# Moving the second batch's scores behind the first products of block 0, in a hand-written order of a sparse attention and feed-forward kernel

## The chip, the cores and the metric

The kernel runs on one core of a Trainium2 chip. The metric is the device time of one execution in microseconds (us); the time of a version is the median of its runs. The engines of the core are TensorE (PE, matrix products), VectorE (DVE), ScalarE (ACT), GpSimd (POOL) and SyncE (SP, here only an issuer of transfers).

## The reference

Sparse attention of 8 batches, 8 heads, 576 tokens of 64 numbers, and then a feed-forward layer on the 4608 tokens of 512 numbers. All is float32.

```python
scores = scale * np.matmul(q, k.transpose(0, 1, 3, 2))
mask_local = (rel >= 0) & (rel < stride)                 # heads 0 to 3
mask_strided = (rel >= 0) & (pos[None, :] % stride == pos[:, None] % stride)   # heads 4 to 7
attn = softmax(np.where(masks, scores, -1e9))
x = np.matmul(attn, v).transpose(0, 2, 1, 3).reshape(B * S, H * D)
h = x @ w_in                                             # 512 x 2048
g = h * (1.0 / (1.0 + np.exp(-h)))
return g @ w_out                                         # 2048 x 512
```

## The kernel before, in words

**Tiling.** The 4608 tokens are cut in nine blocks of 512. A batch's attention is cut in six groups (three of local heads, three of strided heads); group 0 to 5 belong to the first batch, 6 to 11 to the second. Block 0 needs the first batch only. Float32 products of the feed-forward layer are made of three float32r products of split operands (high times high, high times low, low times high).

**Order.** For block 0 every engine's order is written out by hand in the string `PLAN` (line 133), which `Steps.follow` (line 188) reads word by word; each word issues the instructions of one step on one engine. An engine works through its own words in this order and waits where a word needs something that isn't there yet. The words that matter here, with the group or chunk as their number:

- `k` loads keys and queries of a group (line 373, SP queue), `v` its values, `p` a piece of the raw weights into a staging tile (lines 342 and 347).
- `S` makes the scores of a group on PE (line 471; 24 float32 products for a local group, 16 for a strided one, each of which shows as two MATMULs in the trace), `M` adds the mask and takes the maxima on DVE (line 511), `E` the exponentials on ACT (line 529), `R` and `N` sum and scale, `T` transposes on PE (line 554), `P` copies that out (line 558), `O` multiplies with the values (lines 615, 620), `B` copies the result into the block's input x (lines 675, 691).
- `H` and `L` split x into a high and a low part (lines 708, 712), four quarters `00` to `03`.
- `a`, `j`, `b`, `d` turn a raw weight piece into its high and low parts: `a` on ACT (lines 299, 304), `j` on DVE (line 310), `b` on either (line 355), `d` on DVE (line 359).
- `h` and `i` are the first and second half of the products of a chunk of 128 hidden features (line 720, six products of 128 x 512 each); `t` the tanh on ACT (line 730), `g` the gate on DVE (line 752), `w` and `l` the split of the result (lines 760, 764), `o` the output products (line 779).
- `~n` issues idle products: `n` times 128 columns of the identity matrix with itself, into a PSUM bank that nobody reads (line 888).

```python
    def idle(n):
        bank = ps.tile([P, 512], F32, name="ps")
        for i in range(0, n, 4):
            wide = min(4, n - i)
            nc.tensor.matmul(
                bank[:, : wide * P].rearrange("p (i c) -> p i c", c=P), ident,
                ident.unsqueeze(1).broadcast_to([P, wide, P]), start=True, stop=True,
            )
```

**Places.** PSUM has eight banks, four in the ring `ps` and four in `po`. From `ps` a group's scores take two banks until its `M` has read them, a chunk's `h` takes one until its `g` has read it, and idle products take one. A taker gets the bank that has been free the longest. Keys and queries of the second batch lie in two places only (`KBUFS = 2`): groups 6, 8 and 10 use the same place, so `k8` has to wait for `S6` and `k10` for `S8` (in `attention_steps`, `writes=[k_place]`).

Of the kernel before, what the change touches and what calls it, by code (L numbers as in the profile page):

```python
# [132 lines left out]
PLAN = """  # L133
k0 k1 k2 v0 ~7 S0 v1 M0 k4 E0 k3 v2 C0 ~1 S1 k5 M1 E1 ~3 S2 M2 p1 E2 v5 T0 P0.D R1 ~7 S4 O0 R0
M4 E4 Q0 k6 C1 v3 v4 T1 P1.D R2 S3 M3 E3 X0 B0.D a1 T2 P2.D O1 p0 C2 Q1 R4 N4.P S5 M5 k7 O2 X1
Q2 B1.A R3 N3.D S6 k8 j1 T4 P4.A E5 H00.D p3 p4 X2 B2.A M6 T3 P3.D a0 L00.P H01.A O4 p5 p2 O3
b1.D B4 R5 N5.D d1 j0 b0.A L01.P T5 P5.D S8 M8 k10 d0 p6 B3 H02.D L02 O5 B5 H03.D L03 a3 j3
b3.D E6 S7 M7 h0 h1 p7 R6 v7 d3 a5 j5 i0 t0 g0 a2 j2 p9 i1 b5.A d5 w0.D t1 g1 b2.A d2 h2 p11
S10 l0 i2 a6 j6 v6 h3 a7 j7 o0 a4 i3 b6.D w1.D b7.A p8 j4 d7 t2 g2 h4 b4.A d4 l1 o1 k12 p13 a11
N6 p10 w2.A l2 V6 i4 d6 o2 p12 a9 j9 E8 a8 j11 k9 M10 t3 g3 R8 b9.A d9 h5 p15 O6 b11.A d11 a13  # L140
t4 g4 p17 v8 j13 i5 w3.A l3 h6 a10 j10 E10 j8 a12 N8 b8.D d8 o3 p14 w4.A a15 V8 b10.A d10 p16
# [2209 lines left out]
```

## Time and profile before

| | us |
|---|---|
| median of 3 runs | 820.31 (820.23 to 820.51) |
| the profiled execution, its own time | 824.26 |
| its span, first to last instruction | 822.0 |
| PE busy | 811.3 |
| DVE busy | 638.5 |
| ACT busy | 557.5 |
| POOL busy | 74.3 |

The trace's times count from the first instruction of the profiled execution. A row of a timeline gives the start, the length, the engine, the line, what is done and how often, and in brackets the idle time of the engine ahead of it with what ended it; "issue" there is a wait for nothing that the profile shows. The lengths of two neighbouring instructions overlap, so the pitch from one start to the next is the better price of a repeated instruction.

### The profile page before, as it was taken

Reading aid. Unit: us, or ns where it says so; the run is one execution under the profiler, and the core shown is the slowest. Engines: PE = TensorE matmul, PEld = TensorE weight load, DVE = VectorE, ACT = ScalarE, POOL = GpSimd, SP = SyncE. Lnnn points to the kernel's source line nnn. Section 1 sums busy time; section 2 is a strip of 40 time slices with the busy share of each in tenths; the row PEclk is TensorE's granted clock in tenths of the full one; section 3 lists DMA queues with packets and bytes.
Section 4 is the critical chain, followed back from the end, with each engine's and each line's share of the span. In section 5 each row is a group of like instructions: output and inputs, shape, how many; then the busy total and the mean of one; then the engine's idle time right before and its main releaser. Section 6 shows DMA issues by size and latency. Waiting matters only on the chain.

```text
span 822.0 us, 19441 instructions
## 1 busy us (share of the span) xinstructions
PE 811.3 (99%) x7041; PEld 686.5 (84%) x7041; DVE 638.5 (78%) x1571; ACT 557.5 (68%) x1560; POOL 74.3 (9%) x122
## 2 busy tenths in 40 slices
PE   8899999999999999999999999999999999999998
PEld 5688878888898889898988888888888888888887
DVE  6799897787677778786778779676799964789754
ACT  7799876566687678777787769887555624545551
POOL 6300003784000000000000000000000000000000
PEclk9899999999999999999999999999999999999999
DMA  8787354566787876888677877876667697767676
GB/s 270 254 276 253 111 187 127 203 222 237 265 266 252 263 243 210 250 265 264 198 234 247 264 241 242 256 203 181 194 191 219 193 238 227 194 196 194 192 217 156
DMA packets 139007, 182.78 MB, mean 222 GB/s; under 512 B 29408, under 2 KB 82272, under 8 KB 138912
## 3 DMA queue, kind: packets, MB, share of 16 engines
q1 hardware_dynamic: 137392, 180.82, 71.4%
q8 instruction: 56, 0.92, 0.5%
q10 hardware_dynamic: 1520, 0.72, 0.3%
q14 instruction: 39, 0.32, 0.1%
HBM read 142.70 MB, written 38.80 MB: 221 GB/s over the span
## 4 chain that ended last, share of the span: by engine, by line
PE 97%; POOL 1%; issue 1%; DVE 0%; POOLq 0%
PE ps L1549 33%; PE po L779 27%; PE po L2103 13%; PE ps L720 11%; PE ps L2103 4%; PE ps L635 3%; PE po L2232 1%; PE ps L471 1%; PE ps L462 1%; PE po L620 0%; PE po L635 0%; POOL v L399 0%; POOL mask_strided L240 0%; POOL mask__94 L240 0%; PE po L554 0%
## 5 line engine op out<-in xcount | busy, mean ns | idle before, releaser
L1549 PE MATMUL ps<-xop,w 128*128 128x256 f32 (+1 forms) x1152 | 185.5, 310 | 0.0
L1549 PEld LDWEIGHTS ps<-xop,w 128*128 128x128 f32 x1152 | 165.6, 190 | 16.3
L529 ACT ACTIVATE sm<-sm,sums 128x54 f32<-128x54 f32 (+2 forms) x320 | 109.2, 346 | 3.5 <-DVE sums L511 3.4
L720 PE MATMUL ps<-xop,w 128*128 128x512 f32 x384 | 96.5, 400 | 0.0
L1549 PE MATMUL ps<-w,w 128*128 128x512 f32 x384 | 93.7, 389 | 0.0
L779 PE MATMUL po<-w,ghi 128*128 128x512 f32 x280 | 87.1, 392 | 0.0
L720 PEld LDWEIGHTS ps<-xop,w 128*128 128x128 f32 x384 | 72.8, 192 | 15.8
L1549 PEld LDWEIGHTS ps<-w,w 128*128 128x128 f32 x384 | 72.0, 188 | 14.9
L764 DVE TENSOR_TENSOR glo<-th,ghi 128x512 fp32r<-128x512 f32 x80 | 59.3, 743 | 12.4 <-ACT ghi L760 10.5
L529 ACT ACTIVATION_READ_ACCUMULATOR sm<-sm,sums 128x1 f32 x320 | 61.4, 192 | 0.0
L779 PEld LDWEIGHTS po<-w,ghi 128*128 128x128 f32 x280 | 50.4, 189 | 8.9 <-ACT ghi L760 0.2
L760 ACT CAST ghi<-th 128x512 fp32r<-128x512 f32 x78 | 48.3, 621 | 11.8 <-DVE th L752 7.0
L779 PE MATMUL po<-w,glo 128*128 128x512 f32 x140 | 54.6, 390 | 0.0
L779 PE MATMUL po<-stage,ghi 128*128 128x512 f32 x160 | 50.5, 397 | 0.0
L2103 PE MATMUL po<-stage,w 128*128 128x512 f32 x210 | 49.2, 389 | 0.0
L2103 PEld LDWEIGHTS po<-stage,w 128*128 128x128 f32 x210 | 39.4, 188 | 8.2
L602 ACT COPY pt<-sm 32x192 f32<-32x192 f32 (+1 forms) x102 | 36.9, 362 | 5.5 <-DVE sm L594 3.5
L489 POOL MEMSET sm<- 128x80 f32 (+1 forms) x18 | 2.9, 161 | 411.8 <-ACT pt L602 335.0
L1564 ACT ACTIVATE th<-sm 128x512 f32<-128x512 f32 x30 | 18.9, 632 | 29.7 <-DVE sm L1812 24.4
L1942 DVE TENSOR_TENSOR w<-ps,w 128x512 f32<-128x512 f32 x33 | 22.7, 688 | 20.3 <-PE ps L1549 16.3
L2103 PE MATMUL po<-v,w 128*128 128x512 f32 x162 | 38.3, 389 | 0.0
L779 PE MATMUL po<-v,ghi 128*128 128x512 f32 x120 | 38.0, 398 | 0.0
(275 smaller groups left out, 1639.5 us busy)
## 6 DMA issues: line engine op xcount, KB each, us to landing
w<-sums SPq DMA_DIRECT2D x232, 256.0 KB, 3.0
w<-osums SPq DMA_DIRECT2D x104, 256.0 KB, 2.9
sums<-xop SPq DMA_DIRECT2D x16, 512.0 KB, 2.8
osums<-stage SPq DMA_DIRECT2D x16, 512.0 KB, 4.7
v<-vt SPq DMA_DIRECT2D x21, 384.0 KB, 5.3
stage<-w_out SPq DMA_DIRECT2D x14, 512.0 KB, 4.6
k<-kqt SPq DMA_DIRECT2D x14, 477.0 KB, 5.6
stage<-w_in SPq DMA_DIRECT2D x12, 512.0 KB, 4.6
```

The source lines that it names most:

```text
L462: nc.tensor.matmul(self.pss[h][rows, c * WIDE : (c + 1) * WIDE], kbd[at, 1, g.q0[t] : g.q0[t] + 2 * STRIDE], kbd[at, 0, g.k0[t] : g.k0[t] ...
L529: nc.scalar.activation(out=self.s_sb[:, c, h], in_=self.s_sb[:, c, h], func=AF.Exp, bias=self.peaks[:, c, h : h + 1], scale=-1.0, accum_ou ...
L602: nc.scalar.copy(out=self.pt[to, odd], in_=of)
L635: nc.tensor.matmul(self.pso[p][h * D : (h + 1) * D, i * size : (i + 1) * size], vbd[at, 2 * i + h], moved, start=True, stop=True,)
L720: nc.tensor.matmul(ph, weight(0, wi, fc)[:, cc // 2, cc % 2 * P : (cc % 2 + 1) * P], x[xi][cc], start=(cc, n) == (0, 0), stop=(cc, n) == ( ...
L760: copy[engine](out=g[0][:, cols], in_=th[:, cols])
L764: either[engine].tensor_sub(out=g[1][:, cols], in0=th[:, cols], in1=g[0][:, cols].bitcast(F32))
L779: nc.tensor.matmul(po[tt], g[gi][:, cols], weight(1, wi, fc), start=first and n == 0, stop=last and n == 2,)
L1549: nc.tensor.matmul(bank[:, : right.shape[-1]], left(wi, kt), right[:, kt, xi], start=first and (kt, n) == (0, 0), stop=(kt, n) == (1, 2), ...
L1564: nc.scalar.activation(out=th[:, cols], in_=h, func=AF.Tanh, scale=0.5)
L1942: nc.vector.tensor_add(out=to, in0=of(), in1=to)
L2103: nc.tensor.matmul(bank(name, key, m), left[:, wi, m * P : (m + 1) * P], right[xi], start=first and (j, i) == (0, 0), stop=(j, i) == (FH - ...
```

## The change

Two `S`/`M`/`k` triples and one `S`/`M` pair move in `PLAN`, and two idle words are added; no function changes. `S6` is replaced in its old place by `~2` and goes, with `M6` and `k8`, behind `h0`. `S7 M7` goes from ahead of `h0` to behind `i1`. `S8 M8 k10` goes from ahead of `O5` to behind `g1`, and `~4` is put ahead of `O5`. `j3`, `b3.D`, `E6`, `i0` and `i1` change places with their neighbours a little. PE's order becomes `~2 T4 X2 T3 O4 O3 T5 ~4 O5 h0 S6 h1 i0 i1 S7 S8 h2 S10`; before it was `S6 T4 X2 T3 O4 O3 T5 S8 O5 S7 h0 h1 i0 i1 h2 S10`.

```diff
-Q2 B1.A R3 N3.D S6 k8 j1 T4 P4.A E5 H00.D p3 p4 X2 B2.A M6 T3 P3.D a0 L00.P H01.A O4 p5 p2 O3
-b1.D B4 R5 N5.D d1 j0 b0.A L01.P T5 P5.D S8 M8 k10 d0 p6 B3 H02.D L02 O5 B5 H03.D L03 a3 j3
-b3.D E6 S7 M7 h0 h1 p7 R6 v7 d3 a5 j5 i0 t0 g0 a2 j2 p9 i1 b5.A d5 w0.D t1 g1 b2.A d2 h2 p11
+Q2 B1.A R3 N3.D ~2 j1 T4 P4.A E5 H00.D p3 p4 X2 B2.A T3 P3.D a0 L00.P H01.A O4 p5 p2 O3
+b1.D B4 R5 N5.D d1 j0 b0.A L01.P T5 P5.D d0 p6 B3 H02.D L02 ~4 O5 B5 H03.D L03 a3
+h0 S6 M6 k8 j3
+b3.D E6 h1 p7 R6 v7 d3 i0
+a5 j5 t0 g0 i1 S7 M7 a2 j2 p9 b5.A d5 w0.D t1 g1 S8 M8 k10 b2.A d2 h2 p11
 S10 l0 i2 a6 j6 v6 h3 a7 j7 o0 a4 i3 b6.D w1.D b7.A p8 j4 d7 t2 g2 h4 b4.A d4 l1 o1 k12 p13 a11
```

## Rows read from the trace of the kernel before

**Rows 1.** The page: span, busy times of the engines, PE's instruction queue
```profile
span 822.0 us, 19441 instructions
...
PE 811.3 (99%) x7041; PEld 686.5 (84%) x7041; DVE 638.5 (78%) x1571; ACT 557.5 (68%) x1560; POOL 74.3 (9%) x122
...
q8 instruction: 56, 0.92, 0.5%
```

**Rows 2.** Busy time in a stretch: PE, PEld, DVE, ACT, POOL, clock, DMA share, GB/s
```profile
40.00:140.00 100.00, 100.00 (x873) 80.71 (x872) 92.38 (x245) 84.80 (x235) 3.85 (x4) 1.00 0.58 187
```

**Rows 3.** Timeline of PE, 9 to 40 us
```profile
9.25 1.67 PE L888 MATMUL ps<-ident 128*128 128x512 f32 x4
...
16.97 0.35 PE L471 MATMUL ps<-k 64*64 64x64 f32 x8 [1.26 <-issue]
...
18.38 0.72 PE L471 MATMUL ps<-k 64*32 64x64 f32 x48
...
22.16 1.89 PE L620 MATMUL po<-pt,v 64*64 64x54 f32 x57 [0.87 <-issue]
...
24.46 0.72 PE L471 MATMUL ps<-k 64*32 64x64 f32 x48
25.57 0.75 PE L620 MATMUL po<-pt,v 64*64 64x54 f32 x18 [0.39 <-ACT xb L675]
28.69 0.35 PE L620 MATMUL po<-pt,v 64*64 64x54 f32 x2 [2.37 <-issue]
...
30.05 9.31 PE L720 MATMUL ps<-xop,w 128*128 128x512 f32 x30
39.30 0.72 PE L471 MATMUL ps<-k 64*32 64x64 f32 x48
```

**Rows 4.** Busy time in stretches around the stall; the clock is third from the right
```profile
27.00:28.00 1.00, 0.00 (x0) 0.00 (x0) 0.97 (x2) 0.00 (x0) 0.88 (x3) 0.98 1.05 360
...
34.00:35.00 1.00, 1.00 (x4) 0.80 (x3) 0.94 (x2) 0.15 (x1) 0.00 (x0) 0.61 0.12 44
```

**Rows 5.** Chain of work that ended last: six products at the full clock
```profile
51.17 1.36 PE ps L720 x6
```

**Rows 6.** Timeline of DVE, 24 to 34 us
```profile
26.25 0.69 DVE L359 TENSOR_TENSOR w<-stage,w 128x512 fp32r<-128x512 f32 x1
...
27.37 0.69 DVE L712 TENSOR_TENSOR xop<-xb,xop 128x512 fp32r<-128x512 f32 x1
...
32.23 0.21 DVE L511 CUSTOM_DVE_ANT_0 sm<-ps,mask_strided 128x64 f32<-128x64 f32 x1
...
33.38 0.17 DVE L544 TENSOR_SCALAR sums<-sums 128x6 f32<-128x6 f32 x1
```

**Rows 7.** Timeline of POOL, the low part of the second quarter of x
```profile
24.40 1.75 POOL L712 TENSOR_TENSOR xop<-xb,xop 128x512 fp32r<-128x512 f32 x1 [1.96 <-ACT xop L708]
```

**Rows 8.** Timeline of ACT, 25 to 37 us
```profile
25.60 0.92 ACT L675 COPY xb<-po 128x432 f32<-128x432 f32 x1
29.29 0.70 ACT L675 COPY xb<-po 128x306 f32<-128x306 f32 x1 [2.77 <-PE po L620]
...
30.91 0.35 ACT L529 ACTIVATE sm<-sm,sums 128x64 f32<-128x64 f32 x1
...
32.89 0.69 ACT L299 ACTIVATE stage<-stage 128x512 f32<-128x512 f32 x1
...
36.68 0.60 ACT L730 ACTIVATE th<-ps 128x512 f32<-128x512 f32 x1 [2.53 <-PE ps L720]
```

**Rows 9.** DMA issues of the whole span: form, KB each, median us to landing
```profile
k<-kqt SPq DMA_DIRECT2D x14, 416.0 KB, 4.1
...
k<-kqt SPq DMA_DIRECT2D x7, 448.0 KB, 4.7
```

**Rows 10.** DMA issues, 25.5 to 26 us: the load for group 10
```profile
k<-kqt SPq DMA_DIRECT2D x1, 416.0 KB, 6.2
```

**Rows 11.** DMA issues, 160 to 200 us: the quickest load of that size
```profile
k<-kqt SPq DMA_DIRECT2D x1, 416.0 KB, 3.8
```

## The prediction

> **What bounds the kernel now.** I read the busy times first: PE is busy for 811.3 of the 822.0 us of the span, DVE for 638.5, ACT for 557.5 [rows 1]. Then the busy times by stretch: from 40 us on PE shows 100.00 of each 100 us, in nearly every stretch to the end [rows 2]. So what PE loses or saves ahead of 40 us is carried to the end whole. Third comes the timeline of PE up to 40 us, where nearly all its idle time lies: 0.87 us ahead of 22.16, 0.39 ahead of 25.57, 2.37 ahead of 28.69; and the 30 half products that begin at 30.05 end at 39.30 [rows 3], 9.25 us, where 30 x 1.36/6 = 6.80 would do at the full clock [rows 5]. The clock row says why: the granted clock is 0.98 in the stretch 27 to 28 and 0.61 in 34 to 35 [rows 4], which puts the fall to 1.2 GHz near 27.96 and the return to 2.4 GHz near 34.78. At the fall PE had idled since 26.32 (25.57 + 0.75 [rows 3]).
>
> **What the two longer stalls are.** Nothing that the profile shows releases them ("issue"). But between the restart at 22.16 and the next stall lie 57 + 48 + 18 MATMULs [rows 3] and the three transposes of T5, 126 in all, each with its weight load: 252 instructions, and a few waits. PE's instruction queue moved 0.92 MB in 56 packets [rows 1], 16.4 KB each; 2 x 7041 instructions over 56 packets is again 251. So PE ran out of code twice, with the transfer queues full. The Trainium skill ("Runtime: NRT & Kernel Launch", Instruction fetch mechanics) says blocks of 256 instructions, and that crossing a block's end is mostly hidden. The trace agrees with the 256 and not with "hidden". The rival "stalled anyway" below is what the time would be if these stalls belong to their place and not to the count.
>
> **One yardstick.** In both orders PE has the same products ahead of S10 and the same order after it, except six groups of idle columns. S10 starts at 39.30 [rows 3]. The change is worth what it moves S10 by, plus what the clock costs after S10. I follow the new order on the clock of the trace.
>
> **The front, up to h0.** ~2 stands for S6: the seven groups of the old ~7 took 1.67 us [rows 3], 0.24 each, so ~2 is 0.48 against 0.66 (48 MATMULs, 0.72 less the overlap), and ~4 is 0.95; both lie in waits for copies. Taking S6 and S8 (96 instructions each) out and putting two short idle words in moves the code limits back: the second comes 20 products into O3, when by the old times (22.16) the block is there; the third moves from O5 to inside S7. So 0.87 and 2.37 go. DVE loses M6 and M8, 6 x 0.144 each (M7's eight take 33.38 - 32.23 = 1.15 [rows 6]). What ends last then is ACT and POOL: B3 runs 25.60 to 26.52 [rows 8], the cast of weight piece 0 is right ahead of it, so d0 can run 25.7 to 26.4 (0.69) instead of at 26.25 [rows 6]; L01 on POOL ends at 24.40 + 1.75 = 26.15 as before [rows 7]. h0 starts at 26.45, 3.6 us earlier, at the full clock.
>
> **From h0 to S7.** Each half product group is 1.36 [rows 5], S6 0.66: h0 to 27.8, S6 to 28.5, h1 to 29.8, i0 to 31.2, i1 to 32.55, S7 (two thirds of S6) to 33.05. i0 needs the last quarter of x: H02.D and L02 follow B3 (26.95, 27.65; d0 and H02.D took 1.12 together, L02 0.69 [rows 6]), B5 follows B3 and lasts 0.70 [rows 8], H03.D and L03 are done at 28.8. In time.
>
> **S8, the new wait.** S8 needs two banks. h1's is held until g1, S7's two until M7, h0's until g0; so it gets h0's and the first that M7 gives back. M6 queues behind L03 on DVE (28.8 to 29.65); E6 trails it by one maximum and takes 32.89 - 30.91 = 1.98 [rows 8], to 31.05; R6 holds DVE until then. ACT goes on with a5 (two passes of 0.69, to 32.3) and t0 (0.60, to 32.9 [rows 8]); g0 is done at 33.6; half of M7 later, 34.2. S8 runs 34.3 to 34.95, after 1.2 us of idle PE. k8, issued behind S6 at 28.6, lands 4.7 later [rows 9], 33.3: not last. p7 and v7 queue behind k8 on SP, some 1.4 us later than now; their readers come after S10. That costs nothing while they land by then; without that cover it would cost those 1.4.
>
> **S10, the second new wait.** k10 uses the place of group 8's keys, so it leaves after S8, at 35.05. The price of its landing isn't shown for this moment: 3.8 [rows 11] is the quickest of that size, 6.2 [rows 10] is k10's own in the full queue. The moment is a quiet one (DMA share 0.12 at 34 us [rows 4]), so I take the median, 4.1 [rows 9], nearest to the quick end: 39.15, S10 at 39.25. h2 covers 1.36 of that, to 36.3. PE idles 2.95 us. **S10 starts when it did**, with ends -0.4 and +2.0. The 3.6 us at h0 and the 2.45 of slow clock are spent on the S words now behind it (about 1.9), on 1.2 and on 2.95 us of waiting.
>
> **The clock.** The one fall in the trace came after 1.64 us of idling (26.32 to 27.96) [rows 3, 4]; 1.26 us ahead of 16.97 brought none [rows 3]. The new wait of 2.95 is longer than both. If the clock falls in it, it is low when S10 starts; before, it came back 6.1 us after PE resumed (28.69 to 34.78), which at half speed is 3.0 us lost, while the 30 products lost 2.45. I take 2.5. No other idle time ends later: DVE and ACT, which waited more than 2 us each for block 0 (2.77 and 2.53 on ACT [rows 8]), reach l0 and d2 some 3 us earlier than now, so nothing else is late at S10.
>
> **Sum.** 0.0 (S10) + 2.5 (clock) = +2.5. The profiled execution took 824.26 us, 2.26 around its span, and is 3.95 above the median of the runs; I carry only the difference: 820.31 + 2.5 = **822.8**.
>
> **Rivals.**
> - *The clock holds* (0.30). For: half of the time before this wait is dense h2 work, where before the old fall it was small score products. Then only S10 counts: 820.3, between 819.7 and 821.8.
> - *The loads are not last* (0.15), the way to faster. It decides at S8: if S7 and S8 run back to back because S8's banks are not those that M7 frees, S8 ends at 33.7, k10 leaves at 33.8 and at the quick 3.8 S10 starts at 37.7; PE idles 2.6 us at most, and with the clock held that is -1.6 to -2, 818.5. Against: with four banks in the ring I find no other pair.
> - *Stalled anyway* (0.12). The 2.37 us stay at O5 whatever the count. Then h0 starts near 28.8, at half clock as now, the words behind it and k10 follow, S10 comes near 41.5 and the clock falls again: about +4.5, 824.8. Against: the two counts of 252.
>
> **How the numbers follow.** About 0.2% (1.6 us) is what a measurement of this kernel can tell from no change. The forecast has 0.43: 0.38 of it is slower by over that, 0.05 within (S10 a little early and a short slow stretch). The first rival's 0.30 is within but for 0.01 on either side, the second's 0.15 faster, the third's 0.12 slower. Slower: 0.38 + 0.12 + 0.01 = 0.51; within: 0.05 + 0.28 = 0.33; faster: 0.15 + 0.01 = 0.16. The range, 819.0 to 824.8, holds the forecast and the first rival with their ends, the nearest fifth of the second (0.03) and half of the third (0.06), so that 0.18 is left out. The forecast's own range is 821.5 to 824.2.
>
> **What would show it.** Right: h0 at about 26.5 with no "issue" stall ahead of it; a gap ahead of S8 ended by DVE's M7 and one of about 3 us ahead of S10, ended by the DMA of k; a granted clock of 0.5 from about 38 to 45 us, and 1.00 up to it; no PE idle time later. Wrong: "issue" ahead of h0, S8 right behind S7, S10 ahead of 38 us, or a clock of 1.00 throughout.

## The result, and the profile after

The changed kernel took **826.44 us** in the median of six runs (824.81 to 826.76); the kernel before, beside it, 820.41. The ratio is 1.006 (95% interval 1.0046 to 1.0074): slower, by more than was forecast (822.8), and above the range (819.0 to 824.8). The profiled execution of the changed kernel took 824.9 us, its span 822.7, only 0.7 more than the span of before in [rows 1]. That the two profiles differ by 0.7 and the medians by 6.0 is the first thing to explain. The profiled execution of the changed kernel is the second quickest of its six; that of before (824.26) is slower than every one of the six runs beside it (819.82 to 821.86).

The timeline of PE, changed kernel, 24 to 44 us (columns as in [rows 3]; the lines of the kernel's code are two higher than before):

```profile
24.99 0.91 PE L622 MATMUL po<-pt,v 64*64 64x54 f32 x24 [0.25 <-ACT xb L677]
25.83 1.67 PE L722 MATMUL ps<-xop,w 128*128 128x512 f32 x6
27.43 0.72 PE L473 MATMUL ps<-k 64*32 64x64 f32 x48
28.09 4.37 PE L722 MATMUL ps<-xop,w 128*128 128x512 f32 x18
32.39 0.69 PE L473 MATMUL ps<-k 64*64 64x64 f32 x32
33.84 0.87 PE L473 MATMUL ps<-k 64*32 64x64 f32 x48 [0.76 <-DMA k<-kqt]
34.64 1.66 PE L722 MATMUL ps<-xop,w 128*128 128x512 f32 x6
38.64 1.07 PE L473 MATMUL ps<-k 64*32 64x64 f32 x48 [2.34 <-DVE glo L766]
39.64 4.22 PE L722 MATMUL ps<-xop,w 128*128 128x512 f32 x12
43.69 0.62 PE L781 MATMUL po<-w,ghi 128*128 128x512 f32 x2
```

Read against [rows 3]: O5's 24 products run through, with no "issue" stall inside. h0 starts at 25.83 instead of 30.05. Then S6, h1 with i0 and i1 (18 products), S7, a wait ahead of S8, h2, and a wait of 2.34 us ahead of S10. The trace puts that wait down to DVE's `l0`, whose last instruction happens to end at 38.64 too. S10 doesn't read `l0`. It reads the keys of group 10. These two rows of the SP queue give when the loads of `k8` and `k10` left:

```profile
28.21 0.55 SPq L375 DMA_DIRECT2D k<-kqt  x1
...
34.77 0.55 SPq L375 DMA_DIRECT2D k<-kqt  x1
```

and the DMA issues (27.5 to 29 us and 34 to 36.5 us) when they landed, 5.5 us later (33.7) and 3.7 us later (38.5):

```profile
k<-kqt SPq DMA_DIRECT2D x1, 448.0 KB, 5.5
...
k<-kqt SPq DMA_DIRECT2D x1, 416.0 KB, 3.7
```

Both waits end with a load. In other executions of the same kernel the trace names the load ahead of S10 itself (below). The clock falls right behind the wait (busy time by stretch, the clock third from the right, as in [rows 4]):

```profile
38.00:39.00 1.00, 0.36 (x22) 0.39 (x30) 1.00 (x3) 1.00 (x2) 0.00 (x0) 0.90 0.90 308
39.00:40.00 1.00, 1.00 (x47) 0.83 (x31) 1.00 (x3) 0.24 (x2) 0.00 (x0) 0.50 0.96 353
...
42.00:43.00 1.00, 1.00 (x5) 0.83 (x4) 0.00 (x0) 0.50 (x2) 0.00 (x0) 0.89 0.87 311
```

So the fall comes near 38.8, 0.16 us after PE took up S10, and the return near 42.2, which is why the i2 and h3 products behind S10 (12 in 4.22 us) take so long: from S10 to the first output products, o0, it is 5.05 us (38.64 to 43.69). From h0 to the end, PE waits ahead of S8 and S10 and nowhere else.

### The profile page after: what moved, and what is told of

It reads as the page before. It is cut to its first block, busy times and chain, and to the rows that moved or that the text cites. A ratio compares the mean times of both kernels' runs of the same rounds, so it can differ in the third digit from the quotient of the medians.

```text
span 822.7 us, 19454 instructions
## 1 busy us (share of the span) xinstructions
PE 811.3 (99%) x7045; PEld 685.8 (83%) x7045; DVE 640.3 (78%) x1571; ACT 557.8 (68%) x1560; POOL 73.9 (9%) x122
## 4 chain that ended last, share of the span: by engine, by line
PE 96%; DVE 2%; ACT 1%; issue 0%; POOL 0%; POOLq 0%; DVEq 0%; ACTq 0%
PE ps L1551 33%; PE po L781 27%; PE po L2105 13%; PE ps L722 10%; PE ps L2105 4%; PE ps L637 3%; PE ps L473 1%; PE po L2234 1%; PE ps L464 1%; DVE sm L513 1%; PE ps L890 1%; ACT sm L531 1%; PE po L637 0%; DVE xq L661 0%; ACT xb L677 0%
```

## The experiments

Medians differ by a microsecond or two from chip to chip, so every ratio is against runs of before on the same chip.

**The kernel before, once more.** No edit.

> The kernel before once more, unchanged, for the clock and span of each of its runs. Theory A (the profiled execution of before was not a usual one: in most executions the code comes in time at O5, or the clock does not fall, so that S10 starts some 4 us earlier than in the trace shown): the runs that take 820 to 821 us have a span near 818 and a mean granted clock of 0.999 or 1.000, not 0.996, and a new profile shows h0 to h2 at the full clock. Theory B (the 3.95 us between the profiled execution and the median are the price of profiling alone): a new profile shows the 2.37 us stall at O5 and the clock fall again, and the time of a kernel's profiled run lies about 4 us above its median.

820.44 us (12 runs, 819.25 to 824.21), ratio 0.9997 (0.9981 to 1.0013). Its profiled execution spans 818.7, not 822.0. PE's timeline:

```profile
25.46 0.73 PE L471 MATMUL ps<-k 64*32 64x64 f32 x48 [0.57 <-DMA k<-kqt]
26.12 0.78 PE L620 MATMUL po<-pt,v 64*64 64x54 f32 x18
27.92 0.27 PE L620 MATMUL po<-pt,v 64*64 64x54 f32 x2 [1.02 <-issue]
...
28.70 7.09 PE L720 MATMUL ps<-xop,w 128*128 128x512 f32 x30
35.73 0.72 PE L471 MATMUL ps<-k 64*32 64x64 f32 x48
```

The stall sits at the very same instruction, behind the 18th of O5's MATMULs, but lasts 1.02 us, not 2.37. The 30 products run at the full clock, 7.03 us from start to start instead of 9.25. S10 starts at **35.73** instead of 39.30: 1.35 from the front, 2.22 from the clock. Theory A holds for S10. For the clock it doesn't hold as it was put: this execution's mean is 0.997, for the clock was low from 19 to 23 us, among the transposes, where it cost little: S8 behind them waited for its keys all the same. A fall somewhere is usual: on two chips only 15 of 74 runs of before have a mean clock of 0.999 or more (6 of these 12, 9 of the 62 beside the experiments), and among the 62 the ten lowest-clocked runs of one chip (0.995, 0.996) have a median of 822.78, its five highest 820.33. Runs of before reach from 818.48 to 825.5; of 106 in all one took as long as the 824.26 us of the execution that the prediction was worked out from.

**Idle products alone.**

```diff
-... p6 B3 H02.D L02 O5 B5
+... p6 B3 H02.D L02 ~4 O5 B5
```

> The kernel before with one part of the change alone: four groups of idle products ahead of O5. Theory A (PE's clock mostly holds in before anyway): no gain; 0 to +0.9 us for the idle products where nothing hides them. Theory B (the fall of the clock after O5 is usual in before): the clock holds at O5 and the time falls by 2 to 2.5 us.

820.83 us, ratio 0.9986 (0.9973 to 1.0). This fits neither theory's number: not the 2 us, but no loss either; at most a small gain. Its profile has the 30 products in 7.12 us, at the full clock, and S8 late by its load:

```profile
26.41 0.72 PE L471 MATMUL ps<-k 64*32 64x64 f32 x48 [1.25 <-DMA k<-kqt]
27.06 1.12 PE L888 MATMUL ps<-ident 128*128 128x512 f32 x2
...
29.60 7.12 PE L720 MATMUL ps<-xop,w 128*128 128x512 f32 x30
```

In the order of before, then, `k8` can hold up S8 and everything behind it on PE, O5 and h0 included. The first profile didn't show that wait at all. There is no "issue" stall at O5 here: PE reaches O5 only at 28.11.

**S7 alone behind i1.**

```diff
-b3.D E6 S7 M7 h0 h1 ... p9 i1 b5.A d5
+b3.D E6 h0 h1 ... p9 i1 S7 M7 b5.A d5
```

> The kernel before with one part of the change alone: S7 and M7 behind i1, S6 and S8 where they were. Theory A: h0 comes 0.5 us earlier, S7 is done in front of h2 as before, no load waits on it: within 0.5 us of before. Rival (scores behind the first products cost by themselves, through M7 ahead of d5 and g1 on DVE): 1 us or more slower.

822.51 us, ratio 1.0002 (0.999 to 1.0013): the place of S7 costs nothing that can be measured here. Its profiled execution (823.49, the second slowest of its twelve) again has the stall behind the 18th MATMUL of O5, 0.35 us long this time, and the clock low ahead of h0 and in it (25.8 to 32.6):

```profile
26.00 1.31 PE L620 MATMUL po<-pt,v 64*64 64x54 f32 x18
27.66 0.57 PE L620 MATMUL po<-pt,v 64*64 64x54 f32 x6 [0.35 <-issue]
```

**S10 behind h3**, in the changed kernel.

```diff
-S10 l0 i2 a6 j6 v6 h3 a7 j7 o0
+l0 i2 a6 j6 v6 h3 S10 a7 j7 o0
```

> The changed kernel with S10 moved behind h3, so that PE does i2 and h3 (2.7 us) while the keys of group 10 land. Theory A (the loss lies in the wait ahead of S10 and the clock that falls in it): the 2.3 us wait goes, the clock holds, and the time falls from 826.4 by 4 to 6 us, to 820 to 822. Rival (the loss lies elsewhere, in the later transfers or in DVE's longer queue after block 0's start): at most 1.5 us are won, 825 or more.

822.39 us, ratio 1.0007 (0.9995 to 1.0019), where the changed kernel stands at 1.0053 on another chip (next): by the two ratios about 3.8 us of the loss is the wait ahead of S10 and what hangs on it. PE's timeline shows h2, i2 and h3 in one piece and S10 behind them without a wait:

```profile
35.50 4.37 PE L722 MATMUL ps<-xop,w 128*128 128x512 f32 x18
39.80 0.72 PE L473 MATMUL ps<-k 64*32 64x64 f32 x48
```

It is no faster than before, though nothing in it waits for a key load at S10 any more: the 1.9 us of S6, S7 and S8, which in before fill waits of PE, now stand among the dense products, and that is about what h0 gained between this profile and the second one of before (26.55 against 28.70). That sum is argued, not tried apart.

**The changed kernel again.** No edit.

> The changed kernel once more, beside the kernel before, for its difference on this chip and the granted clock of each run. Theory A (before's start varies from execution to execution, the changed one's two waits are always there): slower by 3 to 6 us than before, nearly all runs with a clock of 0.995 to 0.998, the ones at 0.995 and 0.996 some 1.7 us longer than those at 0.998. Rival (the difference of 5 to 6 us was one chip's): within 1.6 us.

826.24 us, ratio 1.0053 (1.0033 to 1.0073). The two waits are there again, and the load ahead of S10 is named:

```profile
34.06 0.30 PE L473 MATMUL ps<-k 64*32 64x64 f32 x2 [0.41 <-DVE th L754]
34.73 0.70 PE L473 MATMUL ps<-k 64*32 64x64 f32 x46 [0.37 <-DVE sums L513]
35.35 1.66 PE L722 MATMUL ps<-xop,w 128*128 128x512 f32 x6
39.92 0.94 PE L473 MATMUL ps<-k 64*32 64x64 f32 x48 [2.91 <-DMA k<-kqt]
```

S8's first product waits for the gate g0 (L754) that frees h0's bank, its second for the maxima of M7 (L513) that free S7's first bank; S10 waits 2.91 us for its keys.

**Without the idle words.**

```diff
-N3.D ~2 j1 ... L02 ~4 O5
+N3.D j1 ... L02 O5
```

> The changed kernel without its two idle words ~2 and ~4. Theory A (both lie in waits, and the clock holds there by the other products): within 0.7 us of the changed kernel, the clock falls ahead of S10 as often. Rival (the idle products cost their 1.4 us, or they keep the clock up at h0): 1.4 us quicker, or 2 us or more slower with a fall at O5 to h1.

825.8 us, ratio 1.0052 (1.0036 to 1.0069): they neither cost nor save anything that can be measured here. h0 starts at 25.68 at the full clock without them.

**S8 early, S6 in its old place.** The loads get time: `S6 k8` stays where it was (M6 behind d0), `S8 M8 k10` comes directly behind h0, `S7 M7` behind i0, against the changed kernel:

```diff
-N3.D ~2 j1 ... d0 p6 ... h0 S6 M6 k8 j3
+N3.D S6 k8 j1 ... d0 M6 p6 ... h0 S8 M8 k10 j3
-v7 d3 i0 / a5 j5 t0 g0 i1 S7 M7 a2 ... g1 S8 M8 k10 b2.A
+v7 d3 i0 S7 M7 / a5 j5 t0 g0 i1 a2 ... g1 b2.A
```

> S6 and k8 back in their old place (M6 behind d0), S8 M8 k10 directly behind h0, S7 M7 behind i0, ~4 kept, ~2 gone. Theory A (the change loses by the chain S6, k8, S8, k10, S10, in which each load starts only when the scores ahead of it are done): k8 is there long before S8 and k10 long before S10, PE doesn't wait from h0 on, the clock holds, h0 starts near 26 and S10 near 34; 1.5 to 2.5 us faster than before, 6 or more faster than the changed kernel. Rival (the scores behind h0 make PE wait for banks, whatever the loads): a wait of 1 us or more ahead of S7 or h2, no faster than before.

819.87 us, ratio **0.9979 (0.9966 to 0.9991)**: faster than before, by about 1.7 us, and about 6 faster than the changed kernel. `k10` now leaves at 28.62, 6.3 us ahead of S10. PE's timeline:

```profile
25.99 1.64 PE L722 MATMUL ps<-xop,w 128*128 128x512 f32 x6
27.56 0.95 PE L473 MATMUL ps<-k 64*32 64x64 f32 x48
28.44 3.01 PE L722 MATMUL ps<-xop,w 128*128 128x512 f32 x12
31.38 0.69 PE L473 MATMUL ps<-k 64*64 64x64 f32 x32
32.01 3.02 PE L722 MATMUL ps<-xop,w 128*128 128x512 f32 x12
34.95 0.72 PE L473 MATMUL ps<-k 64*32 64x64 f32 x48
35.61 3.06 PE L722 MATMUL ps<-xop,w 128*128 128x512 f32 x12
```

No bracket from h0 on: no bank and no load is late. Nine of its twelve runs have a mean clock of 1.000, and they spread less (819.28 to 822.0) than those of before.

**The same without ~4.**

```diff
-L02 ~4 O5
+L02 O5
```

> The same without ~4. Theory A: the idle products lie in O5's wait and only guard the clock; the same time within 0.7 us. Rival (they guard it against a fall that is usual there): 1 to 2.5 us slower in part of the runs, with clocks of 0.996 to 0.998.

819.99 us, 0.9978 (0.9966 to 0.9991): the same. `~4` is not what makes the gain.

**Idle products ahead of S10**, in the changed kernel.

```diff
-d2 h2 p11
+d2 h2 ~8 p11
```

> The changed kernel with eight groups of idle products (about 1.9 us) behind h2, in the wait ahead of S10. Theory A (the wait and the fall of the clock in it are two losses): S10 starts as in the changed kernel, near 39, but the clock holds from S10 on in most runs; 1.5 to 3 us faster than the changed kernel, still 2 to 3 us slower than before. Rival (the fall costs nothing by itself, or comes anyway): the same time as the changed kernel, 4 us or more slower than before.

824.57 us, ratio 1.0049 (1.003 to 1.0067): inconclusive, since the changed kernel was not timed on that chip. In its profile the clock holds behind S10, which still waits 1.70 us for its keys.

**S6 alone back.**

```diff
-N3.D ~2 j1 ... d0 p6 ... h0 S6 M6 k8 j3
+N3.D S6 k8 j1 ... d0 M6 p6 ... h0 j3
```

> The changed kernel with S6 and k8 back in their old place and M6 behind d0; S7, S8 and k10 stay behind the half products. Theory A (what decides is that k10 leaves only a product group ahead of S10): S8 starts about 1 us earlier, S10 waits 2 to 3 us still and the clock falls there; 1 to 2 us faster than the changed kernel, 2.5 us or more slower than before. Rival (what decides is k8 behind S6): the wait ahead of S10 shrinks below 1 us and the time is that of before.

825.51 us, ratio 1.0054 (1.0038 to 1.007): no better than the changed kernel. `k8` is there early, and S8 still starts no earlier than 34.28, for it waits for the banks; `k10` is as late as ever:

```profile
34.28 0.30 PE L473 MATMUL ps<-k 64*32 64x64 f32 x2 [1.65 <-DVE th L754]
34.95 0.70 PE L473 MATMUL ps<-k 64*32 64x64 f32 x46 [0.37 <-DVE sums L513]
35.57 1.66 PE L722 MATMUL ps<-xop,w 128*128 128x512 f32 x6
40.15 1.14 PE L473 MATMUL ps<-k 64*32 64x64 f32 x48 [2.92 <-DMA k<-kqt]
```

The second half of theory A stands (S10 waits 2.92), the first half fell: taking S6 out of the chain doesn't bring S8 forward. So S6's return by itself gains nothing; with `S8 M8 k10` directly behind h0 and `S7 M7` behind i0 as well, the order above is faster than before. `S8 k10` moved by itself, with S6 left behind h0, was not tried.

**The price of the clock, on one chip.** The changed kernel, unedited, and the one with `~8` behind h2.

> The changed kernel, on the same chip as the next one, to take the price of the clock's fall as a difference on one chip. Both theories: 4 to 6 us slower than before, clocks of 0.995 to 0.998.

> The changed kernel with the eight idle groups ahead of S10 again, on one chip with the changed kernel. Theory A (the fall is a loss of its own, half of the 3.4 or 6.8 us that it lasts, only partly hidden): 0.8 to 2.5 us faster than the changed kernel, clocks of 0.998 to 1.000. Rival (after S10 something else, a load or DVE, would hold PE back if the clock didn't): within 0.5 us of the changed kernel though its clock holds.

825.03 us, ratio 1.0047 (1.0028 to 1.0065), and 824.51, ratio 1.0033 (1.0019 to 1.0046); eight of nine runs of the second have a clock of 1.000. The difference is 0.5 us by the medians, 1.1 by the ratios, and the intervals overlap. In its profile S10 still waits for its keys behind the idle products:

```profile
37.17 1.98 PE L890 MATMUL ps<-ident 128*128 128x512 f32 x4
39.53 0.91 PE L473 MATMUL ps<-k 64*32 64x64 f32 x48 [0.38 <-DMA k<-kqt]
```

This pair doesn't give the price of a fall behind S10, for it isn't there in every execution. In the profile of the unedited kernel on this chip the clock fell near 19.4, among transposes. S10 came after the same wait of 2.34 us as in the first profile, and the clock held (timeline, then busy time by stretch):

```profile
41.01 0.82 PE L473 MATMUL ps<-k 64*32 64x64 f32 x48 [2.34 <-DMA k<-kqt]
44.61 0.62 PE L781 MATMUL po<-w,ghi 128*128 128x512 f32 x2
```
```profile
19.00:20.00 1.00, 1.00 (x32) 0.91 (x19) 0.70 (x10) 0.00 (x0) 0.00 (x0) 0.71 1.01 319
...
41.00:42.00 1.00, 0.99 (x49) 0.91 (x50) 1.00 (x3) 0.48 (x1) 0.00 (x0) 1.00 1.11 396
```

From S10 to o0 it took 3.60 us here and 5.05 in the first profile. So the fall costs about 1.5 us where it comes right behind S10, and the late load is the large part of the loss.

## Why the prediction was wrong, and where it was right

**Right: the mechanism up to S10.** h0 was put at 26.45 (25.83 measured), S8 at 34.3 (33.84), S10 at 39.25 (38.64), the wait ahead of it at 2.95 (2.34). From h0 to S10 12.80 us were worked out and 12.81 came. That close an agreement is luck: the products and scores took about 1 us more than was put down and the two waits about 1 us less, and in the two repeats with a profile the same way took 13.51 and 12.94 us. The banks of S8 (h0's, and the first that M7 frees) are the ones that the repeats show. `k8` was said to be not last; in the first profile it was, at 5.5 us to landing instead of 4.7, and S8 still came 0.46 us earlier than worked out.

**Right: the stalls.** The two that the change was said to remove are gone. The second had a fixed place: behind the 18th MATMUL of O5 in both profiles of before and with S7 alone moved, although it lasted 2.37, 1.02 and 0.35 us, and it is not at O5 in the changed order. That fits a count of instructions; that PE ran out of code there is argued from the count and not shown.

**Wrong: the yardstick.** The step that failed is "S10 starts at 39.30 [rows 3]. The change is worth what it moves S10 by", together with "The profiled execution took 824.26 us ... and is 3.95 above the median of the runs; I carry only the difference". The difference was taken from one execution that is not a usual one, and then added to the median of the others. It had the longest stall at O5 that any profile shows and the fall of the clock right ahead of h0; another execution of the same kernel, at 820.94 near its median of 820.44, has S10 at 35.73. Against that the changed kernel's S10 is 2.9, 4.2 and 5.3 us late in its three profiled executions (38.64, 39.92 and 41.01), where 0.0 was put into the sum. (The third lost 2.93 us to an "issue" stall ahead of 18.35, at a place where before lost 1.26 [rows 3].) The 3.95 us were no constant price around the span: the time around it is 2.26 in the first profile of before and 2.24 in the second (824.26 - 822.0, 820.94 - 818.7), and the second took 3.32 less with an S10 that starts 3.57 earlier. So the 3.95 had to lie inside the span, and most of what PE lost ahead of S10 was what I counted as removed by the change.

**Mis-sized: the clock.** 2.5 us were put down. Where the clock fell behind S10 it cost about 1.5 (5.05 against 3.60 from S10 to o0), for it was low for 3.4 us, not 6.1; and it fell not in the wait but behind its end. So the two terms were 0.0 and 2.5 and measured 2.9 to 5.3 and 0 to about 1.5. Together they make the spans of the three profiled executions 4.0, 5.4 and 4.8 us longer than that of before's second (822.7, 824.1 and 823.5 against 818.7). By the ratios the repeats are 3.9 and 4.4 us slower than before and the first comparison 4.9; its medians differ by 6.0, those of the repeats by 2.75 and 4.48, and how much of that spread is chance stays open.

**The rivals.** "The clock holds" came true behind S10 in one of the three profiled executions, but not with its 820.3: that execution took 825.77, for S10 was late. "The loads are not last" needed other banks; the profiles show those that were worked out. "Stalled anyway" is refuted by the timelines: no profile of the changed kernel has the stall inside O5.

## What to carry to other kernels

Before a sum is made against a profile, compare its own time with the median of the runs: where it is longer by more than the change is thought to be worth, ask which of its stalls a usual execution doesn't have, and don't count their removal as gain. Work that moves out of a stage that waits into one that doesn't has to be paid there, so it must bring the later stage forward by more. When a product moves, the load that waits for the place of its operand moves too, so count from that load's start to its first reader. Here the same idea pays when the scores that free a place go in first: four product groups and S7 between `k10` and S10 instead of one group.

## What the runs showed of the hardware that was not expected

One kernel on one core, unchanged, took 818.48 to 825.5 us on several chips, and between its two profiled executions the difference is made in the first 40 us: the "issue" stall at a fixed instruction lasted 2.37 and 1.02 us, and the granted clock fell near 28 us in one and near 19 us in the other. The clock fell among transposes and small score products, in an execution that stayed near the median, as well as ahead of the dense products, where the fall cost 2.2 us (9.25 against 7.03 for the 30 products). After one and the same wait of 2.34 us ahead of S10 it fell in one execution of the changed kernel and held in another. The twelve runs of the order in which no key load or bank is late spread over 2.7 us only.
